# Other loading order for two row groups and a later start of the last step in a layer-norm, 2-D spectral filter and MLP kernel

## The chip, the cores and the metric

The kernel runs on one core of a Trainium2 chip. The core has five engines that run their own instruction streams: TensorE (PE; its weight loads are listed as PEld), VectorE (DVE), ScalarE (ACT), GpSimd (POOL) and SyncE (SP), which here issues every DMA. The metric is the device time of one execution in microseconds (us), median of the runs. Before the change three runs took 372.81, 372.85 and 374.77 us; the median is 372.85 us.

## What is computed

```python
def reference(A_x, A_w_r, A_w_i, B_x, B_w1, B_b1, B_w2):
    ...
    x = A_x                      # (1, 2048, 512)
    xn = _layernorm(x, axis=-1)
    return x + _A_ref(xn, A_w_r, A_w_i) + _B_ref(xn, B_w1, B_b1, B_w2)

    # _A_ref: the spectral branch
        X = jnp.fft.rfft2(x, axes=(-2, -1))
        X = X * (w_r + 1j * w_i)
        y = jnp.fft.irfft2(X, s=(S, D), axes=(-2, -1))
    # _B_ref: the MLP, F = 1792
        h = jnp.einsum("bsd,df->bsf", x, w1) + b1
        act = h * jnp.tanh(softplus(h))
        return jnp.einsum("bsf,fd->bsd", act, w2)
```

(The two branches are shortened to their arithmetic.) Everything is float32 at the boundary.

## The kernel before

**Tiling.** The 2048 rows lie on 128 partitions as row 16p + s, with s from 0 to 15. The sixteen slices s form four groups g of four slices each, 128 rows to a slice. Each product is made of three float16 matmuls (high by high, high by low, low by high; the helper `mm3`, lines 59 to 65), so weights and activations are split into a high and a low half: ACT writes the high half, DVE (or POOL, for the normalized rows) the low half.

**Stages.** (1) The opening (`opening`, line 882) loads group 0's rows and w1, normalizes the rows, turns them on TensorE, makes the first spectral step for its four slices, scales and splits w1, and runs the first fourteen up tiles of the MLP. (2) `middle` (line 1124) runs the down tiles of group 0 between the normalization of groups 1, 2 and 3. (3) A stream of spectral units (`stream_a`) is mixed with the rest of the MLP (`mlp_rest`). (4) In the last step sixteen `s1_inverse` units (line 775), which turn the spectrum back along the rows and add it to the result, are spread between the last MLP tiles.

**MLP.** `up(n)` (L659) makes twelve matmuls of 128x512 into a tile `ph`; ACT then applies the activation (`mish`, L670) and the high half (`a_hi`), DVE the low half (`a_lo`). `down(n)` makes twelve matmuls into four accumulators `pa` (L61, L64, L65, the lines of `mm3`). One call of `up` or `down` counts as one half tile.

**The opening in detail.** `warm` returns `idle`, which issues matmuls on a tile of zeros (`z_w`, L878); `idle(13)` stands ahead of everything. Group 0's rows are loaded into one tile `x_0` by three DMAs (L887): slice 0, slice 1, slices 2 and 3. The DMA of the constants `cTt`, which hold the identity for the turns on TensorE and the first step's matrix, follows, then w1 in seven pieces. For each slice `stats` (L121) and `aggr` (L124) on DVE give mean and variance, `centre` (L145) on ACT subtracts the mean, `root_by_table` gives the reciprocal root for two slices at a time (a square root on ACT, L134; on DVE L136 and L137 make `nk`, L139 to L141 make `rs`), `hi_centred` (L149, ACT) writes the high half from `nk`, `lo_centred` (L153, DVE) the low half from `rs`. TensorE turns both halves (`turn`, L212) and makes the first step (`s1_mm`). After slice 3's low half DVE makes the scale of w1 (L240, L243), ACT splits w1's first piece (`w1_hi`, L304), and the first up tile starts (L659).

**Order.** Opening and middle stand under `tc.manual_schedule()`: on each engine instructions run in the order of the code. After that a scheduler places instructions, except those kept in program order. SP issues DMAs one after another; one that waits for its data holds up those behind it.

**Group 1 and 2.** `row_in` writes a slice's halves; `row_turn` (line 1103) issues a transposing DMA (`turn`, L208, into `xnT`), makes the first step and, every second slice, stores the result to DRAM (`s1_store`, L104). `load_rows(2)` (L860) loads group 2's rows as two DMAs of 512 KB into two of the five buffers of pool `big`, which w2's pieces 0 and 1 used before. The first up tile of group 1 (`act_of(14)`) needs all four transposing DMAs of group 1.

**The last step.** `load_yi` (L772) loads sixteen tiles `yi` of 256 KB that the spectral units have stored through `d_t`. The loop at the end of the kernel lets `T_LAG` half tiles go ahead of the first `s1_inverse`, then spreads all sixteen evenly so that the last stands `T_HOLD` half tiles before the end:

```python
while done[0] - start < T_LAG + k * (total - T_HOLD - T_LAG - start) / (n - 1) and half_tile():
    pass
s1_inverse(*todo.pop(0))
```

`s1_inverse` makes six matmuls into `psY` (pool `f`, two buffers), then DVE adds the result: for group 3, whose four units come first, into `y` (L797), for the others into `m` (L790), which goes out at once (L791). `end_of(s)` (line 737) makes the last accumulators, DVE's L753 and the last stores (L754).

Of the kernel before, what the change touches and what calls it, by code (L numbers as in the profile page):

```python
# [24 lines left out]
N_UNITS = 101  # L25
LAST = 3
B_END = 98
T_LAG = 4
T_HOLD = 2


# [5 lines left out]
def spectral_mlp_kernel(ctx, tc, x, wt, w0, w1, b1, w2, cT, cIT, cM, out):  # L37
    nc = tc.nc
# [14 lines left out]
    xv = x.rearrange("(p s) d -> p s d", s=NS2)  # L53
# [38 lines left out]
    def s1_out(s2, ps):  # L92
        if s2 % 2 == 0:
            y1s[0] = tp.tile([P, 2, 4, 2, P], F16, tag="X", name=f"y1_{s2}", bufs=2)
        y1v = y1s[0][:, s2 % 2]
        psv = ps.rearrange("p (a b) -> p a b", a=4)
        nc.scalar.mul(y1v[:, :, 0, :], psv, 2.0**-17)  # L97
        nc.vector.scalar_tensor_tensor(  # L98
            y1v[:, :, 1, :], psv, 2.0**-17, y1v[:, :, 0, :], op0=ALU.mult, op1=ALU.subtract
        )  # L100

    def s1_store(s2, n=2):
        k = s2 % 2 + 1
        nc.sync.dma_start(  # L104
            d_y1[4 * (s2 + 1 - n) : 4 * (s2 + 1)].rearrange("a p e -> p a e"),
            y1s[0][:, k - n : k].rearrange("p s a h e -> p (s a) (h e)"),
        )
# [277 lines left out]
    def load_wm(c):  # L385
        wmt[c] = big.tile([P, 1024], F32, tag="big", name=f"wm_{c}")
        nc.sync.dma_start(wmt[c], wt[:, c // 2, 1024 * (c % 2) : 1024 * (c % 2) + 1024])

    def load_w0():
        wmt[8] = sp.tile([P, 4, 2, 64], F32, tag="w0t", name="w0t")  # L390
        nc.gpsimd.memset(wmt[8], 0.0)
        for c in range(4):
            nc.sync.dma_start(wmt[8][32 * c : 32 * c + 4], w0[c])

    def max_wm(c):
        if c == 0:
            sc["mxw"] = sp.tile([P, 9], F32, tag="mxw", name="mxw")
        nc.vector.tensor_reduce(
            sc["mxw"][:, c : c + 1],
            wmt[c] if c == 8 else wmt.pop(c),  # L400
            axis=AX.XYZ if c == 8 else AX.X,
            op=ALU.max,
            apply_absolute_value=True,
        )

    def sum_wm():
        mxwa = sp.tile([P, 1], F32, tag="mxwa", name="mxwa")
        nc.vector.tensor_reduce(mxwa, sc["mxw"], axis=AX.X, op=ALU.max)
        sc["am"] = sp.tile([P, 1], F32, tag="am", name="am")
        nc.gpsimd.partition_all_reduce(sc["am"], mxwa, P, bass_isa.ReduceOp.max)  # L410
# [275 lines left out]
    def down(n):  # L686
        g, f = UP[n]
        if f == 0:
            pacc[g] = [ps_a.tile([P, D], F32, tag="a", name=f"pa_{g}_{s}") for s in range(4)]
        a = act.pop(n)  # L690
        for s in range(4):
            mm3(
                pacc[g][s],
                lambda h: a[:, h, s * P : (s + 1) * P],
                lambda h: w2t[:, h, f, :],
                f == 0,
                f == (NFC - 1 - LAST if (g, s) == (3, 3) else NFC - 1),
            )

    def load_res(g):  # L700
        macc[g] = cp.tile([P, 4, D], F32, tag=f"xnT{g}", name=f"m_{g}")
        nc.sync.dma_start(macc[g], xv[:, 4 * g : 4 * g + 4, :])

    def mlp_end(g):

        for s in range(4):
            r = macc[g][:, s, :] if g < 3 else yacc[g][s]
            nc.vector.scalar_tensor_tensor(r, pacc[g][s], sc["out"], r, op0=ALU.mult, op1=ALU.add)
            if g in yacc:
                nc.sync.dma_start(outv[:, 4 * g + s, :], r)  # L710
# [141 lines left out]
    def load_rows(g, tag=None, pool=None):  # L852
        ts = []
        if tag:
            t = (pool or tp).tile([P, 4, D], F32, tag=tag, name=f"x_{g}")
            nc.sync.dma_start(t, xv[:, 4 * g : 4 * g + 4, :])
            return [t[:, s, :] for s in range(4)]
        for a in range(2):
            t = big.tile([P, 2, D], F32, tag="big", name=f"x_{g}_{a}")
            nc.sync.dma_start(t, xv[:, 4 * g + 2 * a : 4 * g + 2 * a + 2, :])  # L860
            ts += [t[:, 0, :], t[:, 1, :]]
        return ts

    def load_ct(g):
        a, b = (0 if g == 0 else P + 1024 * g), P + 1024 * (g + 1)
        nc.sync.dma_start(cTa[:, a:b], cT[:, a:b])
# [4 lines left out]
    def warm():  # L871
        z = tp.tile([P, D], F16, tag="q2", name="z_w", bufs=3)
        nc.gpsimd.memset(z, 0.0)
        ps = ps_f.tile([P, D], F32, tag="f", name="ps_w")

        def idle(n):
            for _ in range(n):
                nc.tensor.matmul(ps, z[:, :P], z, start=True, stop=True)  # L878

        return idle  # L880

    def opening():
        idle = warm()
        idle(13)
        x0 = tp.tile([P, 4, D], F32, tag="z", name="x_0")
        for a, b in ((0, 1), (1, 2), (2, 4)):
            nc.sync.dma_start(x0[:, a:b, :], xv[:, a:b, :])  # L887
        load_ct(0)
        for c in range(7):
            if c < 5:  # L890
# [8 lines left out]
        r = Rows(0, [x0[:, s, :] for s in range(4)])  # L899
# [22 lines left out]
        root = r.root_by_table(0, 2)  # L922
        next(root)
        r.centre(1)
        next(root)
        r.hi_centred(0)
        r.hi_centred(1)
        r.stats(2)
        r.aggr(2)
        r.centre(2)  # L930
        next(root)
# [140 lines left out]
        r = Rows(1, x1)  # L1072
# [25 lines left out]
    def row_in(r, s):  # L1098
        r.hi(s)
        r.full(s)  # L1100
        r.lo(s, POOL)

    def row_turn(r, s):
        s2 = 4 * r.g + s
        r.turn(s)
        ps = s1_bank(s2)
        s1_mm(s2, r.xh[s], ps)
        s1_out(s2, ps)
        if s2 > 13:
            s1_store(s2, 1)  # L1110
        elif s % 2:
            s1_store(s2)

    def act_of(n):
        up(n)
        mish(n)
        a_hi(n)
        a_lo(n)

    def w2_part(c):  # L1120
        w2_hi(c)
        w2_lo(c)

    def middle(r, ps1):
        load_ct(2)
        down(0)
        row_in(r, 0)
        s1_out(0, ps1[0])
        w2_part(2)
        down(1)  # L1130
        row_in(r, 1)
        s1_out(1, ps1[1])
        s1_store(1)
        down(2)
        w2_part(3)
        row_in(r, 2)
        down(3)
        row_turn(r, 0)
        row_in(r, 3)
        w2_part(4)  # L1140
        down(4)
        row_turn(r, 1)
        x2 = load_rows(2)
        down(5)
        row_turn(r, 2)
        w2_part(5)
        down(6)
        row_turn(r, 3)
        r = Rows(2, x2)
        r.stats(0)  # L1150
        r.stats(1)
        w2_part(6)
        down(7)
        r.stats(2)
        r.stats(3)
        down(8)
        nc.sync.dma_start(cMt, cM)
        x3 = load_rows(3, "u")
        load_ct(3)
        act_of(14)  # L1160
        for s in range(4):
            r.aggr(s)
        r.root()
        down(9)
        load_res(0)
        row_in(r, 0)
        act_of(15)
        row_in(r, 1)
        down(10)
        row_turn(r, 0)  # L1170
        act_of(16)
        row_in(r, 2)
        load_wm(0)
        load_wm(1)
        down(11)
        row_turn(r, 1)
        act_of(17)
        row_in(r, 3)
        load_wm(2)
        load_w0()  # L1180
        max_wm(0)
        down(12)
        row_turn(r, 2)
        act_of(18)
        max_wm(1)
        load_wm(3)
        load_wm(4)
        down(13)
        row_turn(r, 3)
        mlp_end(0)  # L1190
        r = Rows(3, x3)
        for s in range(4):
            r.stats(s)
        homes[19] = tp.tile([P, 2, 512], F16, tag="q2", name="a_q2", bufs=3)
        act_of(19)
        down(14)
        for s in range(4):
            r.aggr(s)
        r.root()
        row_in(r, 0)  # L1200
        turn_w0()
        act_of(20)
        row_in(r, 1)
        max_wm(2)
        load_wm(5)
        down(15)
        act_of(21)
        row_turn(r, 0)
        row_in(r, 2)
        max_wm(3)  # L1210
        load_wm(6)
        down(16)
        act_of(22)
        row_turn(r, 1)
        row_in(r, 3)
        max_wm(4)
        load_wm(7)
        down(17)
        act_of(23)
        row_turn(r, 2)  # L1220
        max_wm(5)
        max_wm(8)
        down(18)
        row_turn(r, 3)
        max_wm(6)
        act_of(24)
        max_wm(7)
        sum_wm()
        down(19)
        scale_wm()  # L1230
        return 25, 20

    with tc.manual_schedule():
        n_up, n_down = middle(*opening())
# [13 lines left out]
    for k in range(n):  # L1248
        while done[0] - start < T_LAG + k * (total - T_HOLD - T_LAG - start) / (n - 1) and half_tile():
            pass  # L1250
# [131 lines left out]
```

## Time and profile before

| what | value |
|---|---|
| median of three runs | 372.85 us (372.81 to 374.77) |
| the profiled execution | 373.67 us |
| its span, first to last instruction | 371.9 us |
| mean granted TensorE clock in it | 0.995 |
| busy in it: DVE, ACT, POOL | 250.8 us, 172.0 us, 46.4 us |
| moved by DMA | 55.79 MB, mean 150 GB/s |

Times in the trace count from the span's first instruction. What lies around the span in the profiled execution is 373.67 - 371.9 = 1.8 us. In a timeline row stand start, busy time, engine, line, operation, out<-in, sizes and a count; in square brackets the engine's idle time before it and what ended that. Rows marked SPq are SP's DMA issues: their duration is the issue, not the transfer. A row "DMA out<-in" in the chain of waits goes from the issue to the landing.

### The profile page before, as it was taken

The page shows a single profiled execution, that of the slowest core. Times are in us where ns is not written, and L with a number is a line of the kernel's source. Part 1 is how long each engine was busy: PE and PEld are TensorE (multiplying, and loading weights), DVE is VectorE, ACT ScalarE, POOL GpSimd, SP SyncE. Part 2 cuts the span into 40 slices and gives each one's busy share as a digit, 9 for nine tenths or more (in the row PEclk, how much of TensorE's full clock was granted, in tenths as well). Part 3 has the DMA queues.
Part 4 walks back from the last instruction along what each step waited for, and adds up shares of the span by engine and source line. Part 5 has one row for each costly group of instructions (what it writes and reads, how often), then busy time and mean ns, then how long its engine had stood idle before and what let it go on. Part 6 is the DMA issues. An engine that isn't in the chain of part 4 may idle for free.

```text
span 371.9 us, 5641 instructions
## 1 busy us (share of the span) xinstructions
PE 362.3 (97%) x2085; PEld 185.9 (50%) x2085; DVE 250.8 (67%) x474; ACT 172.0 (46%) x260; POOL 46.4 (12%) x49
## 2 busy tenths in 40 slices
PE   6999999999999999999999999999999999999995
PEld 2644444544544455444555454544555445445654
DVE  4998999554567654589887857787489944314354
ACT  5989968415434443342454354345436354331100
POOL 0020003202204300303030303030030300000000
PEclk9899999999999999999999999999999999999999
DMA  7945512897673498037202370106921234549444
GB/s 240 321 151 182 221 51 62 224 309 260 165 213 105 113 197 280 4 115 275 64 17 64 99 218 4 51 22 195 285 82 45 71 78 115 133 91 358 183 172 169
DMA packets 56156, 55.79 MB, mean 150 GB/s; under 512 B 16144, under 2 KB 44720, under 8 KB 55360
## 3 DMA queue, kind: packets, MB, share of 16 engines
q1 hardware_dynamic: 56128, 55.43, 49.9%
q8 instruction: 16, 0.26, 0.3%
q14 instruction: 12, 0.10, 0.1%
HBM read 35.46 MB, written 12.58 MB: 129 GB/s over the span
## 4 chain that ended last, share of the span: by engine, by line
PE 73%; DVE 12%; DMA 5%; ACT 4%; SPq 2%; issue 2%; POOL 0%; ACTq 0%; DVEq 0%
PE ph L659 28%; PE pa L65 10%; PE pa L64 10%; PE pa L61 10%; DMA xnT<-xh 2%; DVE w2t L374 2%; DMA x<-in_x_dram 2%; DVE w1t L310 1%; ACT w1t L304 1%; DVE q L353 1%; PE psP L470 1%; PE psY L61 1%; PE psY L64 1%; PE psP L480 1%; PE psY L65 1%
## 5 line engine op out<-in xcount | busy, mean ns | idle before, releaser
L659 PE MATMUL ph<-xnT,w1t 128*128 128x512 f16 x672 | 153.5, 379 | 0.6 <-DMA xnT<-xh 0.6
L659 PEld LDWEIGHTS <-w1t 128*128 128x128 f16 x672 | 65.1, 98 | 74.8 <-issue 1.0
L670 ACT ACTIVATE hb<-ph,b1t,fp_exp 128x512 f32<-128x512 f32 x56 | 43.3, 772 | 79.5 <-PE ph L659 79.5
L65 PE MATMUL pa<-w2t,a 128*128 128x512 f16 x181 | 68.6, 379 | 0.0
L61 PE MATMUL pa<-w2t,a 128*128 128x512 f16 x181 | 68.6, 379 | 0.0
L64 PE MATMUL pa<-w2t,a 128*128 128x512 f16 x181 | 68.6, 379 | 0.0
L682 DVE SCALAR_TENSOR_TENSOR a<-hb,ip_a,a 128x512 f16<-128x512 f32 x46 | 36.0, 783 | 35.3 <-ACT a L679 35.1
L679 ACT ACTIVATE a<-hb,ip_a 128x512 f16<-128x512 f32 x46 | 33.1, 719 | 2.2 <-DVE ip_a L243 1.2
L65 PEld LDWEIGHTS <-a 128*128 128x128 f16 x190 | 18.6, 98 | 21.1
L61 PEld LDWEIGHTS <-a 128*128 128x128 f16 x190 | 18.6, 98 | 19.3
L64 PEld LDWEIGHTS <-a 128*128 128x128 f16 x190 | 18.6, 98 | 18.9
L204 POOL TENSOR_TENSOR xh<-xs,xh 128x512 f16<-128x512 f32 x12 | 14.8, 1232 | 64.7 <-ACT xh L188 33.3
L627 DVE SCALAR_TENSOR_TENSOR tt<-psT,tt 128x512 f16<-128x512 f32 x16 | 11.0, 687 | 17.5 <-ACT tt L626 17.5
L485 DVE SCALAR_TENSOR_TENSOR z<-psP,z 128x512 f16<-128x512 f32 x16 | 10.9, 690 | 13.6 <-ACT z L484 13.6
L626 ACT ACTIVATE tt<-psT 128x512 f16<-128x512 f32 x16 | 9.5, 591 | 17.4 <-PE psT L65 13.9
L603 ACT ACTIVATE at<-psA 128x512 f16<-128x512 f32 x16 | 9.4, 590 | 16.9 <-PE psA L65 15.9
L379 ACT ACTIVATE u<-w,sc_u 128x512 f16<-128x512 f32 x16 | 10.8, 713 | 11.2 <-DVE w L579 7.0
L604 DVE SCALAR_TENSOR_TENSOR at<-psA,at 128x512 f16<-128x512 f32 x16 | 11.0, 688 | 7.3 <-ACT at L603 7.2
L188 ACT ACTIVATE xh<-x,nb,rs 128x512 f16<-128x512 f32 x12 | 9.6, 804 | 12.9 <-DVE nb L182 12.9
L484 ACT ACTIVATE z<-psP 128x512 f16<-128x512 f32 x16 | 9.5, 594 | 12.3 <-PE psP L480 12.2
L97 ACT ACTIVATE y<-psS 128x512 f16<-128x512 f32 x16 | 9.4, 588 | 11.4 <-PE psS L65 11.4
L98 DVE SCALAR_TENSOR_TENSOR y<-psS,y 128x512 f16<-128x512 f32 x16 | 11.0, 687 | 5.3 <-ACT y L97 5.3
(205 smaller groups left out, 571.6 us busy)
## 6 DMA issues: line engine op xcount, KB each, us to landing
wm<-in_wt_dram SPq DMA_DIRECT2D x8, 512.0 KB
ai<-at SPq DMA_DIRECT2D x64, 64.0 KB
d_t<-tt SPq DMA_DIRECT2D x32, 128.0 KB
w1s<-in_w_dram SPq DMA_DIRECT2D x7, 512.0 KB
w2s<-in_w_dram SPq DMA_DIRECT2D x7, 512.0 KB
d_y<-y SPq DMA_DIRECT2D x7, 512.0 KB
m<-in_x_dram SPq DMA_DIRECT2D x3, 1024.0 KB
yt<-d_y SPq DMA_DIRECT2D x6, 512.0 KB
```

The lines of the kernel that those rows point to most:

```text
L61: first = nc.tensor.matmul(ps, stat(0), mov(0), start=start, stop=False)
L64: nc.tensor.matmul(ps, stat(0), mov(1), start=False, stop=False)
L65: nc.tensor.matmul(ps, stat(1), mov(0), start=False, stop=stop)
L98: nc.vector.scalar_tensor_tensor(y1v[:, :, 1, :], psv, 2.0**-17, y1v[:, :, 0, :], op0=ALU.mult, op1=ALU.subtract)
L204: engine.tensor_sub(self.xh[s][:, 1, :], self.xs[s], self.xh[s][:, 0, :])
L485: nc.vector.scalar_tensor_tensor(zl, psv, 2.0**-14, zh, op0=ALU.mult, op1=ALU.subtract)
L604: nc.vector.scalar_tensor_tensor(at[:, :, 1, :], ps, 2.0**-15, at[:, :, 0, :], op0=ALU.mult, op1=ALU.subtract)
L627: nc.vector.scalar_tensor_tensor(tt[:, :, 1, :], ps, 2.0**-12, tt[:, :, 0, :], op0=ALU.mult, op1=ALU.subtract)
L659: nc.tensor.matmul(ph[n + k], w1t[:, hw, dc, f * P : (f + 1) * P], xnT[g][:, hx, dc, :], start=(hw, hx, dc) == (0, 0, 0), stop=(hw, hx, dc ...
L670: nc.scalar.activation(hbt[n], ph.pop(n), AF.Mish, bias=b1t[:, f : f + 1], scale=s_exp[part_of(f)])
L679: nc.scalar.activation(act[n][:, 0, :], hbt[n], AF.Copy, scale=sc["a"])
L682: nc.vector.scalar_tensor_tensor(act[n][:, 1, :], hbt.pop(n), sc["a"], act[n][:, 0, :], op0=ALU.mult, op1=ALU.subtract)
```

## The change

The opening's rows come in two loads of two slices instead of three, three more idle matmuls stand ahead, and slice 2's `stats` moves ahead of the second step of the root for slices 0 and 1. The load of group 2's rows moves up, ahead of the first store and of all transposing DMAs of group 1. `T_LAG` goes from 4 to 5.

```diff
-T_LAG = 4
+T_LAG = 5
...
         idle = warm()
-        idle(13)
+        idle(16)
         x0 = tp.tile([P, 4, D], F32, tag="z", name="x_0")
-        for a, b in ((0, 1), (1, 2), (2, 4)):
-            nc.sync.dma_start(x0[:, a:b, :], xv[:, a:b, :])
+        for a in (0, 2):
+            nc.sync.dma_start(x0[:, a : a + 2, :], xv[:, a : a + 2, :])
         load_ct(0)
...
         root = r.root_by_table(0, 2)
         next(root)
         r.centre(1)
+        r.stats(2)
         next(root)
         r.hi_centred(0)
         r.hi_centred(1)
-        r.stats(2)
         r.aggr(2)
...
         down(0)
         row_in(r, 0)
+        x2 = load_rows(2)
         s1_out(0, ps1[0])
...
         row_turn(r, 1)
-        x2 = load_rows(2)
         down(5)
```

What the engines get is seen in the order of the built programs. First VectorE in the opening; `st` and `mv` are the statistics, `ry` and `nk` the root of slices 0 and 1. Before:

```order
L121 BN_STATS st_129<-x_110 128x6
L124 BN_AGGR mv_130<-st_129 128x2
L121 BN_STATS st_129<-x_110 128x6
L124 BN_AGGR mv_130<-st_129 128x2
L136 RECIPROCAL ry_149<-rd_148 128x2
L137 TENSOR_SCALAR nk<-ry_149 128x2
L121 BN_STATS st_129<-x_110 128x6
L124 BN_AGGR mv_130<-st_129 128x2
```

The same place after the change:

```order
L121 BN_STATS st_131<-x_113 128x6
L124 BN_AGGR mv_132<-st_131 128x2
L121 BN_STATS st_131<-x_113 128x6
L124 BN_AGGR mv_132<-st_131 128x2
L121 BN_STATS st_131<-x_113 128x6
L136 RECIPROCAL ry_151<-rd_150 128x2
L137 TENSOR_SCALAR nk<-ry_151 128x2
L124 BN_AGGR mv_132<-st_131 128x2
```

The third BN_STATS, of slice 2, which reads what the second load brings, has moved ahead of L136 and L137, which read only slices 0 and 1.

Second the queue of SP in the middle stage; `d_y` are the stores of the first spectral step, `xnT<-xh` the transposing DMAs of group 1, `x_0` and `x_1` here the two halves of group 2's rows. Before:

```order
L866 DMA cTt<-in_cT_dram 128x1024
L104 DMA d_y_85<-y_0_687 128x8x256
L208 DMA_TRANSPOSE xnT_580<-xh_682 128x8x128
L208 DMA_TRANSPOSE xnT_580<-xh_704 128x8x128
L104 DMA d_y_85<-y_4_751 128x8x256
L860 DMA x_0_784<-in_x_dram 128x1024
L860 DMA x_1_786<-in_x_dram 128x1024
L208 DMA_TRANSPOSE xnT_580<-xh_726 128x8x128
L208 DMA_TRANSPOSE xnT_580<-xh_754 128x8x128
```

After:

```order
L866 DMA cTt<-in_cT_dram 128x1024
L860 DMA x_0_689<-in_x_dram 128x1024
L860 DMA x_1_691<-in_x_dram 128x1024
L104 DMA d_y_85<-y_0_693 128x8x256
L208 DMA_TRANSPOSE xnT_582<-xh_684 128x8x128
L208 DMA_TRANSPOSE xnT_582<-xh_710 128x8x128
L104 DMA d_y_85<-y_4_757 128x8x256
L208 DMA_TRANSPOSE xnT_582<-xh_732 128x8x128
L208 DMA_TRANSPOSE xnT_582<-xh_760 128x8x128
```

The two loads L860 have left the place between the second store and the last two transposes and stand ahead of the first store.

Third VectorE at the end of the program; `m` are the sums of groups 0 to 2, `y` those of group 3, `pa` and `pe` the MLP's last accumulators. Before:

```order
L753 SCALAR_TENSOR_TENSOR y_3499<-pa_1_3050,s_out,y_3499 128x512
L790 SCALAR_TENSOR_TENSOR m_2657<-psY_3725,sc_k,m_2657 128x512
L790 SCALAR_TENSOR_TENSOR m_2657<-psY_3734,sc_k,m_2657 128x512
L753 SCALAR_TENSOR_TENSOR y_3547<-pa_2_3051,s_out,y_3547 128x512
L753 SCALAR_TENSOR_TENSOR y_3547<-pe_3754,s_out,y_3547 128x256
```

After:

```order
L753 SCALAR_TENSOR_TENSOR y_3513<-pa_1_3052,s_out,y_3513 128x512
L790 SCALAR_TENSOR_TENSOR m_2659<-psY_3718,sc_k,m_2659 128x512
L790 SCALAR_TENSOR_TENSOR m_2659<-psY_3727,sc_k,m_2659 128x512
L790 SCALAR_TENSOR_TENSOR m_2659<-psY_3736,sc_k,m_2659 128x512
L753 SCALAR_TENSOR_TENSOR y_3549<-pa_2_3053,s_out,y_3549 128x512
L753 SCALAR_TENSOR_TENSOR y_3549<-pe_3756,s_out,y_3549 128x256
```

Three `m` units instead of two now stand between the last but one and the last full `y`. On TensorE the same shift reads so: of the twelve matmuls of the tile `a_7`, seven stood ahead of the first `psY` before and all twelve do now; each later `psY` stands one place later, and the last one's six matmuls stand after the first of the last nine `pa` matmuls. Elsewhere the order of no engine changes, but for the three added idle matmuls and SP's stores of `m`, which follow DVE.

## The prediction, as put on record before the run

> **What bounds the kernel now.** I read the page first, then who TensorE waited for, then the timeline at each of these waits.
>
> ```profile
> span 371.9 us, 5641 instructions
> PE 362.3 (97%) x2085; PEld 185.9 (50%) x2085; DVE 250.8 (67%) x474; ACT 172.0 (46%) x260; POOL 46.4 (12%) x49
> ...
> PE pt L212 <- DMA cTt<-in_cT_dram: 2.3, 1, 2.3
> PE ps_w L878 <- POOL eps L902: 1.3, 1, 1.3
> PE psY L61 <- DMA yi_z<-d_t: 1.2, 1, 1.2
> PE ph L659 <- DMA xnT<-xh: 0.6, 1, 0.6
> PE psT L61 <- DVE tt L627: 0.2, 1, 0.2
> ...
> 14.72:77.25 62.53, 62.52 (x303) 1.00 0.55 159
> ```
>
> TensorE is busy for 97% of the span; the other engines matter only where they hold it up. The waits of TensorE (us in total, times, longest) name five places. Between 14.72 and 77.25 us there is no gap (62.52 of 62.53 us busy at full clock). So the change can win only at the opening, at the wait for `xnT` and at the wait for `yi_z`; whatever moves the first up tile moves everything behind it by as much, as long as DVE and ACT move with it. This kernel's measurement can tell about 0.5%, 1.86 us of 372.85, from no change.
>
> **The middle: group 2's rows ahead of the transposes.** SP's queue, and the chain of waits to the stall at 77.83:
>
> ```profile
> 62.46 3.50 SPq L208 DMA_TRANSPOSE xnT<-xh  x2
> 67.61 0.39 SPq L104 DMA_DIRECT2D d_y<-y  x1
> 68.05 1.75 SPq L860 DMA_DIRECT2D x<-in_x_dram  x2
> 69.90 5.83 SPq L208 DMA_TRANSPOSE xnT<-xh  x2
> ...
> 71.31 6.38 DMA xnT<-xh
> ...
> 77.83 2.75 PE L659 MATMUL ph<-xnT,w1t 128*128 128x512 f16 x12 [0.58 <-DMA xnT<-xh]
> ...
> 52.27 1.28 DVE L374 SCALAR_TENSOR_TENSOR w2t<-w2s,ip_w,w2t 128x1024 f16<-128x1024 f32 x1
> ```
>
> The first two transposes were issued in 3.50 us, the last two, behind the two loads, in 5.83; the last landed at 71.31 + 6.38 = 77.69, and TensorE sat idle for 0.58 us. Matmuls of 512 columns start every 0.216 us (2.59 us for twelve) while one lasts 0.379, so idle time in this view is 0.16 short of the time lost: 0.74 us. With the loads gone the last two can be issued from 68.05. Even if they took as long as now (69.90 to 77.69, 7.79 us) they would land at 75.84, before TensorE arrives; at the first pair's pace, 3.50 us of issue and the 1.96 from 75.73 to 77.69, at 73.5. **The whole 0.74 us goes.** Next late is nothing near: two to four us of slack.
>
> The loads' own cost: SP reaches them after `load_ct(2)` and waits for the two buffers. The second is free when DVE's L374 of w2's piece 1 ends at 53.55; the next item, the store, was not issued until 61.98 because its data came then. So SP waits at an idle place, and two issues of some 0.9 us (1.75 for both) fit in. Cost nothing; if SP were needed earlier it would be at most these 1.75 us on the first transposes, which by 65.96 + 1.96 = 67.92 land some nine us before use. DVE's statistics of group 2, which read these rows, only become earlier.
>
> **The last step: T_LAG 5.**
>
> ```profile
> 332.60 0.38 PE L61 MATMUL pa<-w2t,a 128*128 128x512 f16 x1
> ...
> 333.90 0.38 PE L61 MATMUL pa<-w2t,a 128*128 128x512 f16 x1
> 335.52 0.28 PE L61 MATMUL psY<-yi_z,cITt 128*128 128x256 f16 x1 [1.24 <-DMA yi_z<-d_t]
> ...
> 332.72 2.75 DMA yi_z<-d_t
> ...
> 362.81 0.75 DVE L753 SCALAR_TENSOR_TENSOR y<-pa,s_out,y 128x512 f32<-128x512 f32 x1 [1.19 <-PE pa L65]
> 363.48 1.40 DVE L790 SCALAR_TENSOR_TENSOR m<-psY,sc_k,m 128x512 f32<-128x512 f32 x2
> ```
>
> The seventh `pa` matmul starts at 333.90, the next could at 334.12, and `psY` starts at 335.52: 1.40 us lost, until the load issued at 332.72 lands 2.75 us later. With all twelve ahead, `psY` is due at 332.60 + 12 x 0.216 = 335.19, so 0.33 us of waiting stays: **1.07 us won**. The load's chain starts in TensorE's own earlier work, so earlier gains shift both alike.
>
> At the end a third `m` unit stands between two `y`. Its `psY` takes the buffer of the unit two before, which DVE frees at the end of the first L790, 363.48 + 0.70 = 364.18; TensorE would be there at 364.13 (its last `psY` there ends its run at 363.92, plus one `pa`). From a signal to TensorE's start it took 0.05 us here (335.47 to 335.52) and 0.14 in the middle (77.69 to 77.83), so it waits **about 0.1 us**; bounds 0 and 0.2. The third L790 takes 0.70 us and ends over 0.9 us before the last full `y` needs DVE, since seven more `pa` matmuls remain: hidden, 0.70 if not. The stores go out at the same distance from the end. Net for this part: -0.97 us.
>
> **The opening: loads, statistics, idle matmuls.**
>
> ```profile
> 0.72 1.35 SPq L887 DMA_DIRECT2D x<-in_x_dram  x3
> 3.69 0.69 DVE L121 BATCH_NORM_STATS2 st<-x 128x6 f32<-128x512 f32 x1 [3.69 <-DMA x<-in_x_dram]
> 4.51 0.66 DVE L121 BATCH_NORM_STATS2 st<-x 128x6 f32<-128x512 f32 x1
> 5.21 0.18 DVE L124 BATCH_NORM_AGGREGATE mv<-st 128x2 f32<-128x6 f32 x1
> 6.01 0.17 DVE L137 TENSOR_SCALAR nk<-ry 128x2 f32<-128x2 f32 x1
> 6.30 1.32 ACT L149 ACTIVATE xh<-xc,nk 128x512 f16<-128x512 f32 x2
> 7.27 0.69 DVE L121 BATCH_NORM_STATS2 st<-x 128x6 f32<-128x512 f32 x1 [1.09 <-DMA x<-in_x_dram]
> 8.00 0.18 DVE L124 BATCH_NORM_AGGREGATE mv<-st 128x2 f32<-128x6 f32 x1
> 8.18 1.01 PE L212 MATMUL pt<-cTt,xh 128*128 128x128 f16 x8 [2.26 <-DMA cTt<-in_cT_dram]
> 9.47 0.29 ACT L134 ACTIVATE rd<-mv,eps 128x2 f32<-128x2 f32 x1 [0.54 <-DVE mv L124]
> 9.99 0.16 DVE L136 RECIPROCAL ry<-rd 128x2 f32<-128x2 f32 x1
> 10.45 0.72 ACT L149 ACTIVATE xh<-xc,nk 128x512 f16<-128x512 f32 x1
> 11.07 1.04 ACT L280 ACTIVATE w1t<-w1s 128x1024 f16<-128x1024 f32 x1
> 12.11 0.70 ACT L149 ACTIVATE xh<-xc,nk 128x512 f16<-128x512 f32 x1
> 12.86 0.75 DVE L153 SCALAR_TENSOR_TENSOR xh<-xc,rs,xh 128x512 f16<-128x512 f32 x1
> 13.95 1.33 ACT L304 ACTIVATE w1t<-w1s,ip_w 128x512 f16<-128x512 f32 x2 [0.24 <-DVE ip_w L243]
> 14.88 15.48 PE L659 MATMUL ph<-xnT,w1t 128*128 128x512 f16 x71
> ```
>
> Let T be when slice 2's statistics start: 7.27 now, when slices 2 and 3 had landed. Then on, in the new order: L136 0.73 later (7.27 to 8.00), `nk` 0.2 behind, the first L149 0.29 behind that (6.01 to 6.30), at T + 1.22. ACT now carries the chain, starting one large instruction every 0.62 us (10.45 to 11.07): L149, L149, slice 2's `centre`, so the second root L134 at T + 3.08; from there to slice 2's L149 0.98 (9.47 to 10.45) but no more wait for DVE in between, T + 4.06; w1's square 0.62 on, slice 3's L149 1.04 on, T + 5.72; DVE's low half 0.75 on, w1's split 1.09 on (12.86 to 13.95), and the up tile when its first half is done, 0.73 on: **T + 8.3**. The old start 14.88 is reached at T = 6.58. The old order had `nk` long before T, so its ACT was ahead; the new one loses 0.7 us at the same T and must win it by an earlier T.
>
> T is not shown, so bounds. Below: DVE cannot start before slices 0 and 1 have passed, 1.70 us (3.69 to 5.39) after the first load lands; it now carries what two did, landed between 3.69 and 4.51; so T is at least 5.4 to 6.2, say 5.9, and the up tile at 14.2, -0.7 us. Above: 7.27, if the second load ends with the same bytes at the same time: 15.6, +0.7. It is issued one issue, 0.45 us (1.35 by three), earlier: 6.82. I take 6.6, between 6.2 and 6.82: **0 us**, ends -0.7 and +0.7.
>
> The three idle matmuls end 0.65 us later, at some 6.6, ahead of any turn: cost nothing. Whether they help hangs on the granted clock:
>
> ```profile
> 4.65:8.06 3.41, 1.27 (x6) 0.48 (x5) 1.80 (x6) 2.83 (x5) 0.00 (x0) 1.00 0.87 263
> 8.06:11.47 3.41, 3.29 (x19) 2.21 (x19) 3.20 (x13) 2.65 (x5) 0.00 (x0) 0.50 1.09 367
> ```
>
> In the first stretch TensorE was busy 1.27 of 3.41 us (the number after the length), and the next was granted a clock of 0.50 (ahead of the last two numbers, the DMA's). With 0.65 more it is 1.92 of 3.41; if that keeps the clock, TensorE has up to 1.6 us more room there. But its room is not the limit: the chain above reaches w1's split at 14.6 by ACT. So 0 us in the forecast; only if T is early does it matter (below). The Trainium skill, "TensorE: Matmul & The Clock Gate", section "What's actually happening", says that the clock falls back after an idle window of about 3.4 us; the trace does not agree, since a pause of 2.26 us was enough. By the page neither pause would cost anything and the added matmuls nothing either; by the row they may; the sum is the same.
>
> **The sum.** 373.67 - 0.74 - 0.97 + 0 = 371.96 against the profiled execution. That one lay 0.82 us over the median of the runs; the two stalls lie where all executions do the same work, so I take them off the median: 372.85 - 1.71 = **371.1 us** (-0.46%).
>
> **The rivals.** *The opening wins* (0.30): two larger loads land early, T near 5.9, and the clock stays: 371.1 - 0.7 = 370.4. At half clock TensorE itself would be the limit: turns from T + 1.9 = 7.8 plus the 6.70 us from 8.18 to 14.88, 14.5, so 370.7. For it: DVE's 1.09 us of waiting for the third load. Against it: the bytes ahead are the same. *The opening loses* (0.12): T stays at 7.27, 371.8. *The wait for `yi_z` returns* (0.08): the load lands 1 us later than 2.75 after its issue, and the half tile hides only that: 372.1. The change then doesn't do what it says there. *Slower than before* (0.05): slice 2's statistics now stand ahead of the root of slices 0 and 1, so a late second load stops what used to run while it was waited for. Each us of T past 6.58 costs one; from T = 8.3 the two gains are eaten, and slower by 0.5% it is from T = 10.2, 374.8. `cTt`, issued behind all of x, was there at 8.18, which speaks against it.
>
> **How the numbers follow.** The forecast has 0.45, of which 0.10 lies beyond the 0.5% mark at 370.99, since it is so close. Faster: 0.30 + 0.10 = 0.40; within 0.5%: 0.35 + 0.12 + 0.08 = 0.55; slower 0.05. The range goes from the first rival's time less half a us for landings I have bounded coarsely, 369.9, to 372.8, where the two losing rivals meet (371.1 + 0.7 + 1.0).
>
> **What would show it.** Right: no wait of L659 for `xnT`; the wait of `psY` for `yi_z` down from 1.2 to some 0.2 us or less; the first L659 between 14.2 and 15.6 and 8.3 us behind slice 2's statistics; granted clock at 8 to 11 us telling of the idle matmuls. Wrong: a new wait of TensorE between 77 and 332, statistics that start past 7.3, or `psY` held up near the end by more than 0.2 us.

## The result and the profile after

The changed kernel takes **370.42 us**, median of seven runs (370.16 to 372.03); beside it seven runs of the kernel before had a median of 373.83 (372.81 to 375.67). The ratio is **0.9912, 95% interval 0.9884 to 0.994**: 0.9% faster, about 3.3 us. The profiled execution took 370.42 us; its span fell from 371.89 to 368.64.

The page of the kernel after, its span and TensorE's busy time:

```profile
span 368.6 us, 5647 instructions
...
PE 362.0 (98%) x2088; PEld 185.0 (50%) x2088; DVE 250.4 (68%) x474; ACT 171.6 (47%) x260; POOL 46.4 (13%) x49
```

Whom TensorE waited for, after (us in total, times, longest):

```profile
PE pt L212 <- ACT xh L149: 1.5, 2, 1.2
PE ps_w L878 <- POOL eps L902: 1.3, 1, 1.3
PE psT L61 <- DVE tt L627: 0.3, 1, 0.3
```

The waits for `cTt`, `xnT` and `yi_z` are gone; in the opening TensorE now waits for ACT's first `xh`. The opening in the timeline after, DVE, ACT and TensorE:

```profile
4.35 0.69 DVE L121 BATCH_NORM_STATS2 st<-x 128x6 f32<-128x512 f32 x1 [4.35 <-DMA x<-in_x_dram]
5.18 0.66 DVE L121 BATCH_NORM_STATS2 st<-x 128x6 f32<-128x512 f32 x1
5.97 0.66 DVE L121 BATCH_NORM_STATS2 st<-x 128x6 f32<-128x512 f32 x1
...
6.73 0.17 DVE L137 TENSOR_SCALAR nk<-ry 128x2 f32<-128x2 f32 x1
...
7.00 1.33 ACT L149 ACTIVATE xh<-xc,nk 128x512 f16<-128x512 f32 x2
...
7.78 0.40 PE L212 MATMUL pt<-cTt,xh 128*128 128x128 f16 x4 [1.25 <-ACT xh L149]
...
8.85 0.28 ACT L134 ACTIVATE rd<-mv,eps 128x2 f32<-128x2 f32 x1
...
9.65 0.70 ACT L149 ACTIVATE xh<-xc,nk 128x512 f16<-128x512 f32 x1
...
13.14 1.34 ACT L304 ACTIVATE w1t<-w1s,ip_w 128x512 f16<-128x512 f32 x2 [0.23 <-DVE ip_w L243]
...
13.91 23.84 PE L659 MATMUL ph<-xnT,w1t 128*128 128x512 f16 x109
```

Slice 2's statistics start at 5.97 without any wait (7.27 before, after 1.09 us of waiting for the third load), and the first up tile at 13.91 instead of 14.88: **0.97 us** won. The granted clock over the two stretches that the prediction showed (TensorE's busy time stands behind the length, the clock ahead of the last two numbers):

```profile
4.65:8.06 3.41, 2.16 (x13) 0.90 (x11) 3.20 (x13) 2.63 (x5) 0.00 (x0) 1.00 1.03 366
8.06:11.47 3.41, 3.10 (x33) 2.19 (x31) 2.90 (x10) 3.41 (x8) 0.00 (x0) 1.00 1.09 353
```

TensorE was busy for 2.16 us of the first instead of 1.27, and the second was granted 1.00 instead of 0.50.

SP's queue and TensorE's arrival in the middle, after:

```profile
49.70 3.37 SPq L860 DMA_DIRECT2D x<-in_x_dram  x2
...
61.62 3.52 SPq L208 DMA_TRANSPOSE xnT<-xh  x2
66.78 0.40 SPq L104 DMA_DIRECT2D d_y<-y  x1
67.27 4.09 SPq L208 DMA_TRANSPOSE xnT<-xh  x2
...
76.25 2.75 PE L659 MATMUL ph<-xnT,w1t 128*128 128x512 f16 x12
```

The issue of the loads now takes 3.37 us instead of 1.75, but at a place where SP was waiting anyway. The last pair of transposes was issued in 4.09 us instead of 5.83, and the tile at 76.25 carries no bracket: nothing was waited for.

The last step after, SP's load of `yi_z`, then TensorE around the first `psY`, then DVE and TensorE where the third `m` unit was added:

```profile
330.85 1.76 SPq L772 DMA_DIRECT2D yi_z<-d_t  x4
331.12 0.38 PE L61 MATMUL pa<-w2t,a 128*128 128x512 f16 x1
...
333.50 0.38 PE L65 MATMUL pa<-w2t,a 128*128 128x512 f16 x1
333.71 0.27 PE L61 MATMUL psY<-yi_z,cITt 128*128 128x256 f16 x1
...
359.93 1.40 DVE L790 SCALAR_TENSOR_TENSOR m<-psY,sc_k,m 128x512 f32<-128x512 f32 x2
360.37 0.38 PE L61 MATMUL pa<-w2t,a 128*128 128x512 f16 x1
360.73 0.27 PE L61 MATMUL psY<-yi_w,cITt 128*128 128x256 f16 x1
361.58 0.75 DVE L790 SCALAR_TENSOR_TENSOR m<-psY,sc_k,m 128x512 f32<-128x512 f32 x1 [0.25 <-PE psY L65]
```

From 333.50 to 333.71 is one step of the matmul's pace: `psY` lost nothing (1.40 us before). At the end `psY` could have started at 360.37 + 0.22 = 360.59 and did at 360.73: 0.14 us of new wait.

Where the span's 3.24 us came from, each counted by the starts of TensorE's rows:

| place | before | after | won |
|---|---|---|---|
| first up tile starts | 14.88 | 13.91 | 0.97 |
| lost at the tile that reads `xnT` | 0.74 | 0 | 0.74 |
| lost at the first `psY` | 1.40 | 0 | 1.40 |
| lost at the added third `psY` of the end | 0 | 0.14 | -0.14 |
| small losses elsewhere (one up tile at 37.38, one `psT`) | 0.35 | 0.58 | -0.23 |
| from TensorE's end (368.01, 365.25) to the span's end | 3.88 | 3.39 | 0.49 |

(The rows sum to 3.23; 0.01 is rounding.) The forecast had the second and third row and the fourth; it had nothing for the first and the last. The table is the account of one pair of executions; in the medians of several the gain is shared out otherwise (below).

### The profile page after: what moved, and what is told of

It reads as the page before. It is cut to its first block, busy times and chain, and to the rows that moved or that the text cites. A ratio compares the mean times of both kernels' runs of the same rounds, so it can differ in the third digit from the quotient of the medians.

```text
span 368.6 us, 5647 instructions
## 1 busy us (share of the span) xinstructions
PE 362.0 (98%) x2088; PEld 185.0 (50%) x2088; DVE 250.4 (68%) x474; ACT 171.6 (47%) x260; POOL 46.4 (13%) x49
## 4 chain that ended last, share of the span: by engine, by line
PE 93%; DVE 2%; DMA 2%; SPq 1%; ACT 1%; issue 0%; ACTq 0%; DVEq 0%
PE ph L659 39%; PE pa L64 13%; PE pa L65 13%; PE pa L61 13%; PE psP L470 1%; PE psY L61 1%; DMA x<-in_x_dram 1%; PE psY L64 1%; PE psP L480 1%; PE psY L65 1%; PE psT L61 1%; DMA ai<-at 1%; PE psT L65 1%; PE psT L64 1%; PE psA L61 1%; PE psA L64 1%
```

## The experiments

Two theories stood against each other after this result. **Parts add up**: three independent edits, and the opening's two loads bring most of the gain. **Order or clock**: the loads alone do little, and the moved statistics, or the idle matmuls by way of the granted clock, bring the opening's gain. Later two questions came up: why two loads are early, and why the end behind TensorE's last matmul got shorter. Each run is compared with runs of the kernel before on the same chip; their medians lay between 373.83 and 374.47 us.

**The kernel before once more.** No edit; its profile shows how much of a stall belongs to one execution.

> The kernel before once more, for its opening. Theory A (three loads regularly end late): slice 2's statistics start at 7.0 to 7.4 us again, the granted clock falls to 0.5 in the stretch around 8 to 11 us, the first up matmul (L659) starts at 14.5 to 14.9. Theory B (the profiled execution was an accident): statistics at 5.6 to 6.4 us, clock 1.0, first up matmul at 13.5 to 14.0, so that the opening of the change wins nothing on average. The waits at xnT (0.5 to 0.7 idle) and yi_z (1.0 to 1.4 idle) are there in both.

374.64 us. From its waits and its opening:

```profile
PE pt L212 <- DMA cTt<-in_cT_dram: 2.8, 1, 2.8
PE psY L61 <- DMA yi_z<-d_t: 1.6, 1, 1.6
```

```profile
8.31 0.69 DVE L121 BATCH_NORM_STATS2 st<-x 128x6 f32<-128x512 f32 x1 [2.09 <-DMA x<-in_x_dram]
...
9.11 1.01 PE L212 MATMUL pt<-cTt,xh 128*128 128x128 f16 x8 [2.77 <-DMA cTt<-in_cT_dram]
...
15.77 1.46 PE L659 MATMUL ph<-xnT,w1t 128*128 128x512 f16 x6
```

The third load is later still (8.31), the loss at `psY` larger (1.63 idle), and the wait for `xnT` so short (0.07 idle) that the view doesn't list it. Both theories of the expectation are off: the opening is later than either had it, and the stall at `xnT` that both took for granted is nearly gone. The profile of before, from which I had worked, had a long `xnT` stall and a mild opening.

**T_LAG alone, the load of group 2's rows alone, the opening alone**, each put into the kernel before:

```diff
tlag5:         -T_LAG = 4
               +T_LAG = 5
x2_early:      +        x2 = load_rows(2)   (behind row_in(r, 0))
               -        x2 = load_rows(2)   (behind row_turn(r, 1))
opening_only:  the hunks in opening(), without the other two
```

> Before, with T_LAG 5 alone. Theory A (gains of three places add up, since TensorE alone bounds): the wait for yi_z is gone or under 0.4 idle, the wait for xnT stays at 0.5 to 0.7, a new one of 0.1 at the third psY near the end; time -1.0 to -1.3 us (-0.3%). Rival (the stall only moves: the next psY or the last stores become late): another wait of 0.5 us or more behind 332 us, time within 0.3 us of before.

> Before, with group 2's rows loaded ahead of the first store alone. Theory A: the transposes of group 1 land near 74 us, no wait for xnT, yi_z wait as before, time -0.75 us (-0.2%). Rival (the transposes were slow by themselves or SP was held at the load): they land within 1 us of 77.7, the wait for xnT stays over 0.4 idle, time unchanged.

> Before, with the three edits of the opening alone. Theory A: statistics of slice 2 start near 6.0, clock 1.0 at 8 to 11 us, first up matmul near 13.9, time -0.5 to -1.0 us. Theory B (the early landing and the clock were luck): first up matmul anywhere from 13.9 to 15.6, time within 0.3 us of before. The waits at xnT and yi_z stay.

| kernel | median us | ratio (95%) | slice 2's statistics | first up tile | idle before the first `psY` | up tile to TensorE's end |
|---|---|---|---|---|---|---|
| before (the profile shown) | 374.33 beside the next three, 373.83 beside the last | | 7.27 | 14.88 | 1.24 | 353.13 |
| tlag5 | 374.15 | 0.9993 (0.9977 to 1.0009) | 6.62 | 15.78 | 0.22 | 351.58 |
| x2_early | 373.54 | 0.9987 (0.9970 to 1.0004) | 8.27 | 16.54 | 1.03 | 352.06 |
| opening_only | 372.08 | 0.9944 (0.9925 to 0.9963) | 5.97 | 13.91 | 0.85 | 352.16 |
| after | 370.42 | 0.9912 (0.9884 to 0.9940) | 5.97 | 13.91 | 0 | 351.34 |

The opening alone carries -0.56%, 2.1 us, twice the 0.5 to 1.0 us expected; it starts its up tile at 13.91, just as the whole change does. That is more than the 0.97 us of the two profiles shown, because the opening of the one before was a mild one: its up tile started at 14.88, those of before_again, tlag5, x2_early and before_one_more (below) between 15.57 and 16.54. The mean of these five profiles is 15.71, 1.80 later than 13.91. T_LAG alone and the load alone can't be told from no change by time, though their profiles show what they were to do. For the load that agrees with the 0.75 us expected (0.5 us, interval -0.15 to 1.1). For T_LAG it doesn't: 1.0 to 1.3 us were expected, and the interval ends at 0.9 us. Where the time went that the profile shows as won stays open. (The wait for `xnT`, expected to stay, happened to be gone in that profile.) In tlag5 these are the waits of TensorE:

```profile
PE pt L212 <- DMA cTt<-in_cT_dram: 2.6, 1, 2.6
...
PE psY L61 <- DMA yi_z<-d_t: 0.2, 1, 0.2
```

The 0.22 us that stay idle at `psY` are the remainder that the prediction expected (0.33 lost). In x2_early no wait for `xnT` is left, but its opening was as late as any (8.27). The ratios multiply to 0.9944 x 0.9987 x 0.9993 = 0.9924, against 0.9912 measured: the parts add up within their intervals, and most of the sum is the opening.

**Which edit of the opening.** Each of its three edits is taken back in the kernel after; one further run is the kernel after itself.

```diff
after_idle13:       -        idle(16)
                    +        idle(13)
after_stats_old:    r.stats(2) back behind r.hi_centred(1)
after_three_loads:  -        for a in (0, 2):
                    +        for a, b in ((0, 1), (1, 2), (2, 4)):
```

> The change once more. If its opening is regular: both loads landed by 4.5 and 5.8, clock 1.0 at 8 to 11 us, first up matmul at 13.8 to 14.1, no waits for xnT and yi_z, new waits under 0.2 us each at the third psY near the end and near 37 us. If it was luck: one of these late by 0.5 us or more.

> After, with 13 idle matmuls instead of 16. Theory C (the idle matmuls keep the clock): TensorE is busy only some 1.5 of 3.41 us in the stretch before 8 us, the granted clock falls to 0.5 for the next 3.41 us, TensorE becomes the limit of the opening and the first up matmul comes at 14.4 to 14.9 instead of 13.9; time +0.5 to +1.0 us against the change. Rival (they do nothing, DVE and ACT set the start): clock 1.0 or 0.5, the first up matmul stays within 0.2 us of 13.9.

> After, with slice 2's statistics back behind the root's second step. Theory D (prediction's chain: with the statistics ahead, nk comes 0.3 us later and ACT carries the chain): nk starts near 6.5 instead of 6.73, first up matmul 0.1 to 0.3 earlier, near 13.7. Rival (DVE would idle at the root's wait for ACT and lose it later): first up matmul 0.2 to 0.5 later, near 14.2.

> After, with the old three loads. Theory E (the third load as such ends late, 7.2): statistics of slice 2 start at 7.2, first up matmul at 15.2 to 15.6 as the prediction's T + 8.3 has it; time +1.0 to +1.7 us against the change. Rival (late only by chance): first statistics at 3.7, slice 2's at 5.4 to 5.7, first up matmul at 13.3 to 13.9, no slower than the change.

| kernel | median us | ratio (95%) | slice 2's statistics | first up tile | granted clock at 8 to 11 us |
|---|---|---|---|---|---|
| after_again (one run) | 370.45 | | 6.29 | 14.23 | 1.00 |
| after_idle13 | 370.80 | 0.9912 (0.9889 to 0.9934) | 6.09 | 14.03 | 1.00 |
| after_stats_old | 370.70 | 0.9901 (0.9878 to 0.9923) | 7.03 | 14.48 | 1.00 |
| after_three_loads | 372.93 | 0.9954 (0.9936 to 0.9972) | 8.01 | 15.98 | 1.00 |

Only the loads make a difference that the time shows: with the old three the kernel is 0.4% slower than with two. (The up tile of after_again came 0.32 us behind that of the kernel after, between what its two theories gave.) With the third load the statistics wait again, longer than theory E had it (7.2):

```profile
4.42 0.66 DVE L121 BATCH_NORM_STATS2 st<-x 128x6 f32<-128x512 f32 x1
8.01 0.69 DVE L121 BATCH_NORM_STATS2 st<-x 128x6 f32<-128x512 f32 x1 [2.71 <-DMA x<-in_x_dram]
```

The idle matmuls make no difference that can be measured: with thirteen the time is the same, and all six executions had a mean granted clock of 1.00. The profile of that run doesn't test theory C, though. Here are the idle matmuls of the kernel after and of after_idle13:

```profile
1.30 5.22 PE L878 MATMUL ps_w<-z_w 128*128 128x512 f16 x16 [1.30 <-POOL eps L902]
```

```profile
1.30 5.68 PE L878 MATMUL ps_w<-z_w 128*128 128x512 f16 x13 [1.30 <-POOL eps L902]
```

Thirteen lasted longer than sixteen. They start 0.427 us apart until the first record of a granted clock in the trace; in the kernel after that record begins at 4.57, and from then on they start 0.216 apart. In after_idle13 it begins only at 6.79, when all thirteen had started. So TensorE was idle there for just 0.92 us ahead of the first turn, and the nearly idle stretch that theory C needs didn't occur.

The order of the statistics makes no measurable difference either: with the old order the up tile starts 0.57 us later in the profile, of which 0.28 belongs to the first load, on which DVE began at 4.63 instead of 4.35. The other 0.29 goes against theory D, which had the old order earlier.

The clock is not needed for the loss: the profile of after_three_loads kept 1.00 and was late all the same. But it has a share in it. Nine of that run's twelve executions had a mean granted clock of 0.995, as most of the kernel before have, and took 372.71 to 373.48 us; one at 0.998 took 373.01, the two at 1.00 took 370.86 and 372.05. Late loads and half clock come together there, so this doesn't part them. And with the old order the up tile follows slice 2's statistics by 7.45 us in after_stats_old at full clock and by 7.46 in before_again and before_one_more (below) at half clock, but by 7.61 in before, 8.27 in x2_early and 9.16 in tlag5. In tlag5 the constants for the first turn landed only at 8.96, and from the turn at 9.00 to the up tile the chain of waits runs through TensorE alone; it was busy for the whole stretch that was granted half clock:

```profile
9.11:12.52 3.41, 3.41 (x21) 2.28 (x20) 3.18 (x10) 3.08 (x6) 0.40 (x1) 0.50 1.09 357
```

So of "Order or clock" the order falls and the idle matmuls with it; late loads cost time by themselves, and half clock adds to it in some executions. How the 0.4% divides between the two was not measured.

**Why two loads are early.** In every profile with the loads of before (six: before, before_again, tlag5, x2_early, after_three_loads, before_one_more) the trace's sixteen landing signals of the third load show half of the engines done by 5.5 to 5.8 us and the last at 6.6 to 8.3; with two loads of two slices the last is there by 5.6 to 6.0. The constants behind the rows are late with them: their last engine landed at 8.1 to 9.1 with those three loads and at 6.3 to 6.7 with the two. In tlag5 it was the constants that set the opening, since its third load was there by 6.6. Two other splits of the same bytes, in the kernel after:

```diff
after_small_first:  for a, b in ((0, 1), (1, 4)):
after_large_first:  for a, b in ((0, 2), (2, 3), (3, 4)):
```

> The kernel after, with group 0's rows in two loads of one and three slices instead of two and two. Count theory (a third load of rows is what lands late, because each load more puts one more packet train on every one of the 16 DMA engines ahead of the rest): two loads, nothing late; slice 0 starts early (st near 3.7), slices 1 to 3 land by about 5.6 to 6.0, statistics of slice 2 between 5.9 and 6.4, first up tile 13.9 to 14.4, median as after (370.2 to 371.2). Small-first theory (the load of one slice with its short 2 KB rows puts one engine behind): the load of three slices lands late on one engine, at 7 to 8.3, and since slice 1 is in it now too, the statistics of slice 1 start only then; first up tile 15.5 to 16.5, median 372 to 373.5. Granted clock at 8 to 11 us: 1.00 if the first, open if the second.

> The kernel after, with group 0's rows in three loads of two, one and one slices. Count theory: the third load (slice 3) or the constants behind it land late on one engine, at 7 to 8.3; slice 2 is in the second load and may be on time (T 5.9 to 6.6), but slice 3's statistics or the first turn move to 7.5 to 9.5 and the first up tile to 14.8 to 16; median 371 to 372.9. Small-first theory: no small load goes first, so nothing is late: all rows by 6.0, first up tile 13.9 to 14.4, median 370.2 to 371.2, as after.

after_small_first took 371.55 us, 0.9913 (0.9893 to 0.9934); after_large_first 370.78 us, 0.9899 (0.9871 to 0.9926). Statistics in the first:

```profile
3.61 0.69 DVE L121 BATCH_NORM_STATS2 st<-x 128x6 f32<-128x512 f32 x1 [3.61 <-DMA x<-in_x_dram]
...
5.79 0.69 DVE L121 BATCH_NORM_STATS2 st<-x 128x6 f32<-128x512 f32 x1 [1.27 <-DMA x<-in_x_dram]
...
6.62 0.66 DVE L121 BATCH_NORM_STATS2 st<-x 128x6 f32<-128x512 f32 x1
```

and in the second:

```profile
4.47 0.69 DVE L121 BATCH_NORM_STATS2 st<-x 128x6 f32<-128x512 f32 x1 [4.47 <-DMA x<-in_x_dram]
...
6.09 0.66 DVE L121 BATCH_NORM_STATS2 st<-x 128x6 f32<-128x512 f32 x1
...
7.45 0.69 DVE L121 BATCH_NORM_STATS2 st<-x 128x6 f32<-128x512 f32 x1
```

The three slices behind a small first load landed in time, at 5.79, so the small-first theory falls. But slice 1 is among them, so slice 2's statistics start at 6.62 and the up tile at 14.56, 0.65 later than in the kernel after; these and the 371.55 us lie above what the count theory gave. Three loads as such do the rows no harm either when the large one goes first: nothing waits behind 4.47, the up tile starts at 14.03, and the times that the count theory gave for this kernel were wrong too. One thing of it remains. In after_large_first the constants behind the rows were late on some engines (median signal 6.5, last 7.63; in the kernel after the last came at 6.34), and nobody noticed, since the first turn waited for ACT until 7.89. So in every profile with three loads some engine fell behind between some 6 and 8 us, and the order of the loads decides whose data it holds. What makes an engine fall behind stays open.

**The end behind TensorE.** All kernels so far with the early load of group 2's rows ended 3.32 to 3.39 us behind TensorE's last matmul, the four with the late load 3.88 to 4.63. The trace has a fetch of instructions, one packet of 8 KB on queue 14, 1.55 to 1.88 us behind TensorE's end in those four, while the last store is on its way; in the others it falls behind the end of the span. One DMA instruction more on SP should shift it:

```diff
-                nc.sync.dma_start(b1t, b1)
+                nc.sync.dma_start(b1t[:, :7], b1[:, :7])
+                nc.sync.dma_start(b1t[:, 7:], b1[:, 7:])
```

> The kernel before, with the load of w1's bias (b1, 128x14) split into two loads of 7 columns: one more DMA instruction in SP's stream, early and off every path. Fetch theory (the last store of the program lands 0.5 to 1.3 us late where a fetch of instructions, 8 KB, falls beside it; one instruction more on SP moves that fetch to another place): the fetch is moved from 1.6 to 1.9 us behind TensorE's end by at least 0.5 us or past the end of the span, and the time from TensorE's end to the span's end falls from 3.88 to 4.19 to about 3.4. Rival, the place of the load of group 2's rows or the order of the last stores decides: 3.8 to 4.6 us as in all four kernels with that load in the old place. If the fetch doesn't move at all, it belongs to another engine than SP, and the run says nothing of the two. Opening and the stalls in the middle and the last step as in before (slice 2's statistics 6.6 to 8.3).

> The kernel after, with the load of w1's bias split into two loads of 7 columns: one more DMA instruction in SP's stream, as in before_one_more. There it moved the fetch of instructions from 1.57 us behind TensorE's end to 0.75 us ahead of it, 2.3 us earlier in the program, and the time from TensorE's end to the span's end fell to 2.96. Fetch theory: in the kernel after, where the fetch came 3.70 us behind TensorE's end and beyond the span, the same instruction brings it to about 1.4 us behind TensorE's end, where the last store is under way; one engine of that store lands 0.5 to 1.6 us late, and the time from TensorE's end to the span's end rises from 3.39 to between 3.8 and 4.6; median 0.4 to 1.2 us over that of after (370.4), 370.8 to 371.7. Rival, the early load of group 2's rows or the order of the last stores makes the short end: it stays at 3.3 to 3.5, and the fetch falls where it likes. Opening and middle as in after (slice 2's statistics near 6.0, first up tile near 13.9, no wait for psY).

| kernel | us | fetch, from TensorE's end | last store: 15th and 16th engine landed | TensorE's end to span's end |
|---|---|---|---|---|
| before | 373.67 (this execution) | +1.56 | 370.06, 370.93 | 3.88 |
| before_one_more (one run) | 372.59 | -0.75 | 369.87, 369.88 | 2.96 |
| after | 370.42 | +3.70 | 367.30, 367.32 | 3.39 |
| after_one_more | 370.99, 0.9912 (0.9882 to 0.9941) | +1.56 | 367.21, 368.36 | 4.18 |

The queues from TensorE's end to the span's end, in before_one_more:

```profile
q1 hardware_dynamic: 513, 0.40, 41.2%
```

and in after_one_more:

```profile
q1 hardware_dynamic: 515, 0.40, 29.9%
q14 instruction: 1, 0.01, 1.0%
```

SP's last wait, for the last stores, in the kernel after and then in after_one_more:

```profile
SPq L1378 <- DMA out_dram<-y: 1.2, 2, 0.7
```

```profile
SPq L1379 <- DMA out_dram<-y: 2.3, 3, 1.6
```

The same harmless instruction shortens the end of one kernel and lengthens that of the other, as the fetch leaves the last store or meets it. That shows the fetch's place as the cause, by one profile in each direction; the rival, the place of the load or the order of the stores, had it the other way both times. That the late engine is the one that carried the fetch isn't recorded, and why the early load shifts the fetch was not tried. Nor is the end of the kernel after free of loss: where the fetch falls behind the span's end (eight profiles), DVE's last drain instruction starts 0.38 to 0.41 us after ACT's, in the other six 0.02 to 0.03 after it. So the 2.96 of before_one_more is shorter than the 3.39 of the kernel after and the 3.4 expected; whether the fetch causes this too was not tried. In time the two can't be told apart: 370.99 against 370.42, with intervals of 0.3% on either side. The Trainium skill, "Runtime: NRT & Kernel Launch", section "Instruction fetch mechanics", says that the sequencer streams its instructions through a DMA queue of its own and that crossing a block costs little, mostly hidden; here the one fetch beside the last store cost 0.8 to 0.9 us of span, and what the others cost was not asked.

No version beat the kernel after by more than the intervals.

## Why the prediction was right in direction and short in size

The forecast was 371.1 us, 1.7 below the kernel before; 370.42 lies in its range, and the gain was about twice as large. It was also made of other parts: the forecast had all of it from the two stalls and nothing from the opening, and the runs show 2.1 us for the opening alone, 0.5 and 0.3 for the two edits against stalls, neither of them clear of no change. That 370.42 meets the first rival's 370.4 is luck, since that time starts from 372.85, and the seven runs beside the result gave 373.83.

- **"The whole 0.74 us goes"** (the middle): right for this pair of profiles, and the loads cost nothing where they now stand. But the size was that of one execution: at the old place the loss was 0.74, 0.23 (before_again), 0.29 (opening_only), 0.26 (before_one_more) and 0 (tlag5). A fair term would have been 0.3, the mean of the five; x2_early's interval holds 0.3 and 0.74 alike. The step that failed is the reasoning that this stall lies where all executions do the same work.
- **"1.07 us won ... 0.33 us of waiting stays"** (the last step): the profiles show the mechanism, the time of tlag5 doesn't confirm the size (above). In tlag5 0.22 us idle stayed, as worked out. In the kernel after none did, since the load of `yi_z` was issued 0.27 us before the first of the twelve `pa` matmuls (330.85, 331.12) and not 0.12 after it (332.72, 332.60). In the profiles with T_LAG 4 TensorE sat idle there for 0.79 to 1.63 us.
- **"About 0.1 us" at the third `psY`**: 0.14. The third L790 is hidden, as said.
- **The opening, "0 us, ends -0.7 and +0.7"**: the mis-sized term. The chain held: forecast T + 8.3, measured 13.91 - 5.97 = T + 7.94. It was 0.36 too long because `nk` came 0.76 and not 0.93 behind T, and slice 2's L149 0.80 and not 0.98 behind its root. What failed was T, taken as 6.6 between 6.2 and 6.82 on the reasoning that the same bytes end at about the same time. T was 5.97, where the prediction's lower bound had it, since not the bytes but one late engine of a third load had set 7.27. The first rival, with T near 5.9 and the clock kept, is what happened. The prediction also had the new order lose 0.7 us at the same T; after_stats_old gives 0.49 (T + 7.45), but there T came 2.40 behind the first statistics and not 1.62, so that the new order is ahead.
- **The idle matmuls, 0 us; SP's moved loads, 0 us**: right.
- **The clock: TensorE's room "is not the limit"**: the changed kernel kept the clock, so its runs don't test it. In the kernel before it was right for before_again and before_one_more, not in general: in x2_early and tlag5 the up tile started 1.59 us behind ACT's split of w1, against 0.77 to 0.78 in every profile at full clock.
- **What the sum left out**: the 0.49 us behind TensorE's end. The prediction said that the stores go out at the same distance from the end, and they do (0.47 us behind it before, 0.46 after); what changed is whether a fetch of instructions met the last one. No edit aimed at that, so it is luck.

Against the small losses that came up elsewhere (0.23 us), opening and end give 0.97 + 0.49, and the remainder at `psY` 0.33: these make up the 1.5 us between forecast and result in this pair of executions.

## What to carry to other kernels

When a consumer waits for the last of several small loads, look at how far apart the engines of that load land before reasoning from bytes: here the split of 1 MB of rows into loads of two slices was worth 0.4% (taken back) to 0.6% (with the rest of the opening, alone), and the two edits against stalls from the list of waits 0.2% by themselves, not clear of no change. Take the size of a stall from more than one execution, since the same stall ran from 0 to 0.74 us. Of three edits that are worth 0.9% together, two may be too small to measure alone. And before a run is read as a test, see whether its profile has the condition that the theory needs: the one with thirteen idle matmuls hadn't.

## What the runs showed of the hardware that was not expected

The granted clock. The records change in steps of 3.41 us. Here is before_again:

```profile
5.50:8.91 3.41, 0.83 (x4) 0.29 (x3) 0.94 (x3) 2.13 (x4) 0.00 (x0) 1.00 0.95 299
8.91:12.32 3.41, 3.21 (x19) 2.08 (x19) 3.19 (x13) 2.46 (x5) 0.00 (x0) 0.50 1.09 360
```

and after_three_loads:

```profile
5.38:8.79 3.41, 1.54 (x7) 0.49 (x5) 0.76 (x2) 0.91 (x2) 0.00 (x0) 1.00 0.94 316
8.79:12.20 3.41, 2.15 (x21) 1.47 (x21) 2.98 (x12) 3.14 (x6) 0.00 (x0) 1.00 1.09 358
```

A stretch in which TensorE was busy 0.83 us of 3.41 (0.84 in tlag5, 1.24 to 1.27 in three others) was followed by half clock, one with 1.54 was not, although the pause in it was longer (2.92 us, against 2.26 in before). So the length of the whole pause doesn't decide. The busy share of the stretch sorts these six (24% to 37% was followed by half clock, 45% wasn't), but so does the longest idle time inside the stretch (1.97 us and more against 1.87), and which of the two counts isn't shown. The Trainium skill, "TensorE: Matmul & The Clock Gate", section "What's actually happening", gives a free-running window of 3413 ns, which these steps agree with. What half clock costs depends on who is the limit: nothing in before_again, where ACT's chain was, and some 0.8 us in x2_early, where TensorE was (1.59 us against 0.78 behind ACT's split of w1).

The others were told above: a first record of granted clock that comes anywhere between 4.27 and 7.23 us, with matmuls 0.427 us apart ahead of it and 0.216 behind it; a load whose last engine lands 0.9 to 2.7 us behind its median one when the rows come as one, one and two slices, and a fetch of instructions beside the last store, which held the program's end by 0.8 to 0.9 us.
